# Attention and a token-mixing MLP in one stream: max tiles moved from the projection stretches to the first MLP product

## The chip, the cores and the metric

The kernel runs on one core of a Trainium2 chip. The metric is the device time of one execution in microseconds (us). All engines of the core take part: TensorE (PE; its weight loads are shown as PEld), VectorE (DVE), ScalarE (ACT), GpSimd (POOL) and SyncE (SP), which issues the transfers.

## The reference

The output is a gated sum of two branches over the same x of 2048 tokens by 640 channels, in float32.

```python
g = sigmoid((x * gate_w).sum(-1, keepdims=True))
# branch A: 32 query heads of width 20 on one shared key and value head
q = (x @ wq).reshape(B, S, 32, 20).transpose(0, 2, 1, 3); k = x @ wk; v = x @ wv
p = softmax(einsum("bhqd,bkd->bhqk", q, k) * 20 ** -0.5)
a = einsum("bhqk,bkd->bhqd", p, v).transpose(0, 2, 1, 3).reshape(B, S, 640) @ wo
# branch B: an MLP along the token axis, F = 1728
h = layernorm(x)
u = gelu(einsum("bsd,sf->bdf", h, w1) + b1)
b = (einsum("bdf,fs->bds", u, w2) + b2).transpose(0, 2, 1)
return g * a + (1 - g) * b
```

## The kernel before

The matmuls run on float32 operands split into a high and a low part, so most products are three matmuls (high by high, low by high, high by low), and the contraction is often cut into two halves of 64 rows. PE then works as two row halves side by side; the text calls each a lane. Two matmuls on different lanes run at the same time.

The kernel first projects q, k and v and normalizes x (up to line 438). Then `mix_kernel` writes out by hand one stream of stretches for the rest. A **visit** is one key block of 128 tokens for one unit of four heads and 512 queries; there are 32 units of 16 visits, 512 visits. A visit has four score tiles (`qk`, the matmul of line 700, 512 columns, two per lane), each followed by an exp on ScalarE (line 709) from PSUM to SBUF, and a PV group (`pv_group`, line 735: per visit eight records of 32 output columns). Before a unit's scores come its row maxima: 64 **max tiles** per unit (`ms_next`, the matmul of line 488 with a `tensor_reduce` on VectorE, line 494); they are gathered per unit by `ms_done`, and stored and fetched through DRAM (`store_max`, `fetch_max`). They need no exp and belong to no visit, so they can stand anywhere ahead of their unit.

A **stretch** is what stands between two PV groups: scores and max tiles, and **filler** matmuls of 320 columns from the MLP or the output projection. The filler of a stretch goes on one lane, and most scores and maxes on the other; the next stretch swaps the lanes. The list `ph` holds the filler of every stretch in order:

- the first MLP product, `b1_jobs` (line 986): 84 stretches of 24 filler matmuls, the first of them without visits; each output tile takes four stretches, then `gelu` on ScalarE and GpSimd in steps that `settle` hands out;
- the second product, `b2_jobs` (line 802): 16 row tiles of eight stretches with 20 or 21 fillers;
- the output projection, `a_jobs` (line 931): `NA` blocks of four stretches with 15 fillers;
- the tail: the last `TAIL` visits in `BLOCKS` of two, with no max tiles; here the remaining blocks of the projection are done by `tail_job` (line 886), whole ones first, then those of the last 512 queries for the heads that are ready.

`visits` says how many visits end each stretch (0, 1 or 2). In a stretch the order of score (s) and max (m) tiles on the one lane and around the filler (F) on the other is a letter pattern by visits and filler count (`PATTERN`), shortened or lengthened to a number of max tiles that `shares` hands out. `main` then merges both lanes by planned durations and the planned time at which a PSUM bank comes free. Seven banks rotate among scores, maxes and PV sums (three "ms", three "s", one "o"); an eighth, "g", holds the filler's sum. Outside the tail each PV group's sum is copied from PSUM by ScalarE (line 747) and added by GpSimd (line 748); in the tail it stays in its bank.

The weights w1 and w2 come in chunks of up to four row groups of 128 (`w1_load`, four raw buffers), and `w1_upto` splits each with two GpSimd operations (lines 126 and 127, four split buffers). All transfers named here are issued by SP, in program order. `tail_load` fetches operands of the tail's projection into room that the MLP has left.

Of the kernel before, what the change touches and what calls it, by code (L numbers as in the profile page):

```python
# [27 lines left out]
NU = NQB * NQ  # L28
PRO = 7
LEAD = 46  # L30
TAIL = 24
BLOCKS = (2,) * 12
NA = 10
NP = 12
EPS = 1e-5
GC = math.sqrt(2.0 / math.pi)
# [4 lines left out]
def mix_kernel(ctx: ExitStack, tc: tile.TileContext, A_x, A_wq, A_wk, A_wv, A_wo,  # L41
               B_x, B_w1, B_b1, B_w2, B_b2, gate_w, out):
    nc = tc.nc
    x = A_x[0]
# [39 lines left out]
    HS = NS // 4  # L84
    chunks = [(fc, hf) for d in range(2) for fc in range(FC) for hf in range(4)]
    W2 = len(chunks)
    chunks += [(st, hf) for st in range(NS) for hf in range(4)]
    w1t = {}
    fetched = [0]

# [2 lines left out]
    def w1_load(n):  # L93
        while len(w1raw) < min(n, len(chunks)):
            c = len(w1raw)
            wr = w1r.tile([P, HS, P], F32, name="wr")
            if c < W2:
                fc, hf = chunks[c]
                rows = slice(hf * HS * P, (hf + 1) * HS * P)
                for o in range(0, P, P if fc < FC - 1 else FT):  # L100
                    fw = P if fc < FC - 1 else FT
                    nc.sync.dma_start(out=wr[:, :, o:o + fw],
                                      in_=B_w1[rows, fc * P:fc * P + fw].rearrange("(c p) f -> p c f", p=P))
            else:
                st, hf = chunks[c]
                cols = slice(st * P, (st + 1) * P)
                nf = min(HS, FC - 1 - hf * HS)
                nc.sync.dma_start(out=wr[:, :nf, :],
                                  in_=B_w2[hf * HS * P:(hf * HS + nf) * P, cols].rearrange("(c p) s -> p c s", p=P))
                if nf < HS:  # L110
                    for o in range(0, P, FT):
                        nc.sync.dma_start(out=wr[o:o + FT, nf, :], in_=B_w2[(FC - 1) * P:, cols])
            w1raw[c] = wr

    def w1_upto(n):
        while fetched[0] < min(n, len(chunks)):
            c = fetched[0]
            w1_load(c + 1)
            wr = w1raw[c]
            wh = w1p.tile([P, HS, P], F32R, name="wh")  # L120
            wl = w1p.tile([P, HS, P], F32R, name="wl")
            nv = min(HS, FC - HS * chunks[c][1]) if c >= W2 else HS
            if c < 4 * PRO + 4:
                nc.scalar.activation(wh, wr, AF.Copy)  # L124
            else:
                nc.gpsimd.tensor_copy(wh[:, :nv], wr[:, :nv])
            nc.gpsimd.tensor_sub(wl[:, :nv], wr[:, :nv], f32(wh[:, :nv]))  # L127
            w1t[c] = wh, wl
            fetched[0] += 1
            w1_load(c + 4)  # L130
# [19 lines left out]
    qtiles, qmax = {}, {}  # L150
# [18 lines left out]
    with tc.tile_pool(name="pa", bufs=1) as pa, \  # L169
# [622 lines left out]
    def b2_jobs(st):  # L792
        hold = {}

        def mm(fc, k, d, half):
            if not hold.get("n"):
                hold["p"], hold["n"] = ps_g.tile([P, NB], F32, name="g"), 0
            wh, wl = w1t[W2 + 4 * st + fc // HS]
            w, u = ((wh, u_hi), (wh, u_lo), (wl, u_hi))[k]
            hold["n"] += 1  # L800
            r = slice(64 * half, 64 * half + 64)
            other_tile(half, nc.tensor.matmul(hold["p"][:, :HD2], w[r, fc % HS, :], u[d][r, fc, :],  # L802
                             start=(hold["n"] == 1), stop=(hold["n"] == 6 * FC - 3)))
# [12 lines left out]
        def steps(d):  # L816
            full = [[(fc, k), (fc, k)] for fc in range(FC - 1) for k in range(3)]
            return [[lambda fc=fc, k=k, h=h: mm(fc, k, d, h) for h, (fc, k) in enumerate(f)]
                    for f in full + [[(FC - 1, 0), (FC - 1, 1)], [(FC - 1, 2)]]]

        return (lambda: None), [(steps(d), lambda d=d: done(d)) for d in range(2)]

# [172 lines left out]
    def batches(tiles, counts):  # L995
        out = []
        for n, (load, parts, *_) in enumerate(tiles):
            for d, (steps, done) in enumerate(parts):
                cnt = counts.pop(0)
                rows = [[f[h] for f in steps if len(f) > h] for h in range(2)]  # L1000
                cut = [[len(r) * j // cnt for j in range(cnt + 1)] for r in rows]
                for j in range(cnt):
                    rest = []
                    if d == 0 and j == 0 and n + 1 < len(tiles):
                        rest.append(tiles[n + 1][0])
                    out.append(([r[c[j]:c[j + 1]] for r, c in zip(rows, cut)], rest, [done] if j == cnt - 1 else []))
        return out
# [11 lines left out]
    for st in range(NS):  # L1019
        ph += stretches(batches([b2_jobs(st)], [2] * 2))  # L1020
        if st < NS - 1:
            for k, n in ((-3, 1), (-1, 4)):
                ph[k][1].append(lambda c=W2 + 4 * (st + 1) + n: w1_upto(c))
    ph[-1][1].append(second)
    for c in range(DC):
# [2 lines left out]
    aj = [a_jobs(st) for st in range(NA)]  # L1028
    ph[-8][1].append(aj[0][0])
    ph += stretches(batches(aj, [1] * 2 * NA))  # L1030
    visits = [0] + [2] * (len(ph) - 4 * NA - 1)
    left = len(units) - TAIL - sum(visits)
    visits += [1] * (8 * NA - left) + [2] * (left - 4 * NA)
    assert len(visits) == len(ph)
    early = NS - 4 - NA + 4
    for i in range(early):
        ph[len(ph) - 3 - 2 * (early - 1 - i)][1].append(lambda i=i: tail_load(i))
# [14 lines left out]
    sent, back_in = {0}, {0}  # L1052

    AHEAD, DRAIN, ENTER, FIRST = 4, 0.19, 0.138, 0.1
    PATTERN = {(2, 24): ("smsmsssmsmmsmmms", "F"), (2, 20): ("smsmssmmsmmssm", "mFs"), (2, 15): ("smsmsssmsmmss", "mFmm"),
               (1, 15): ("msmmssms", "F"), (0, 24): ("mmmmmmmssss", "Fs")}

    def pattern(k):
        return PATTERN[visits[k], min((n for n in (15, 20, 24)), key=lambda n: abs(n - len(ph[k][0])))]

    def shares():
        base = [sum(x.count("m") for x in pattern(k)) for k in range(len(ph))]
        total, got, at = 64 * NU - sum(given), [], 0
        for k in range(len(ph)):
            at += base[k]
            got.append(total * at // sum(base))
        return [e - s for s, e in zip([0] + got, got)]

    lanes = [0.0, 0.0]
    fresh = [True, True]  # L1070
# [7 lines left out]
    def main(k, vs, n_max):  # L1078
# [5 lines left out]
        xs, side = pattern(k)  # L1084
        before, after = side.split("F")
        need = end + AHEAD - sc[b]
        n_m = n_max - (before + after).count("m")
        while xs.count("s") < need:
            i = len(xs) * 2 // 3
            xs = xs[:i] + "s" + xs[i:]  # L1090
        while xs.count("s") > need and xs.count("s") > 0 and vs and need >= 0 and (k + 1 < len(ph)):
            i = xs.rindex("s")
            xs = xs[:i] + xs[i + 1:]
            break
        while xs.count("m") < n_m:
            xs += "m"
        while xs.count("m") > max(0, n_m):
            i = xs.rindex("m")
            xs = xs[:i] + xs[i + 1:]
        xs, before, after = list(xs), list(before), list(after)  # L1100
        while sc[1 - b] + (before + after).count("s") < end:
            before.append("s")
        total, count = len(xs) + len(before) + len(after) + len(fs), 0
        while fs or after or before or xs:
            if count == (total + 1) // 2:
# [24 lines left out]
        settle(len(vs) == 2)  # L1130
        if vs:
            n, kb = units[vs[0]][0] + 1, units[vs[0]][1]
            if n in kept and n not in back_in:
                fetch_max(n)
                back_in.add(n)
        for f in rest:
# [14 lines left out]
    pool.append((0.0, ps_o.tile([P, NB], F32, name="o")))  # L1151
    v = 0
    clock.update(now=0.0, act=0.0, dve=0.0, pv=0.0)
    share = shares()
    for k in range(len(ph)):
        n = visits[k]
        main(k, list(range(v, v + n)), share[k])
        v += n
        if k == len(ph) - 4:
            raw = last_wo()  # L1160
        if k == len(ph) - 2:
            w_last = split_last(raw)
# [130 lines left out]
```

## Time and profile before

| what | value |
|---|---|
| median of 3 runs (lowest, highest) | 1635.69 us (1635.39, 1635.93) |
| profiled execution | 1635.82 us |
| its span | 1634.0 us |
| ScalarE, GpSimd: share of the span | 80%, 53% |
| DMA | 135.88 MB, mean 83 GB/s |
| VectorE max tiles (line 494, largest group) | 682 ns each |
| ScalarE exps (line 709, largest group) | 619 ns each |

The span is the time from the first to the last instruction of the profiled execution; the rest of its 1635.82 us lies around it. A mean duration on VectorE or ScalarE runs from start to end of one instruction, and the next one may start before that, so the distance of starts has to be read from the order of time. A matmul's recorded duration also overlaps its neighbours'; a row with "x2" merges two. In the order of time a bracket gives the idle time ahead of an instruction and what ended it.

### The profile page before, as it was taken

How to read it: one execution, taken by the hardware profiler on the slowest of the kernel's cores; microseconds unless marked ns; L12 is line 12 of the kernel's file. 1: busy time of each engine (PE TensorE's matmuls, PEld its weight loads, DVE VectorE, ACT ScalarE, POOL GpSimd, SP SyncE). 2: the span in 40 equal slices, each digit the busy share in tenths (PEclk: the TensorE clock that was granted, in tenths of full speed). 3: DMA queues.
4: the chain of work that ended last, by engine and by line, in shares of the span. 5: the costliest groups of instructions: out<-in, count | busy, mean ns of one | idle time of the engine just before them, and what ended most of it. 6: DMA issues, size and time to landing. Idle time of an engine off the chain costs nothing.

```text
span 1634.0 us, 39357 instructions
## 1 busy us (share of the span) xinstructions
PE 1623.5 (99%) x14877; PEld 1133.6 (69%) x14877; DVE 1395.2 (85%) x2396; ACT 1304.3 (80%) x2579; POOL 873.2 (53%) x986
## 2 busy tenths in 40 slices
PE   9999999999999999999999999999999999999998
PEld 7899667767677676666666666666666666666666
DVE  6689888888888888888898998999888898799943
ACT  4445888888888888888888888888888888888885
POOL 6568677777787777434444444544344443433320
PEclk9999999999999999999999999999999999999999
DMA  7655222222332222122221222112222212334321
GB/s 214 209 164 145 65 79 78 73 66 69 86 82 71 79 74 69 38 65 73 65 72 52 71 64 70 57 45 57 65 65 64 65 54 85 102 97 144 117 79 40
DMA packets 173603, 135.88 MB, mean 83 GB/s; under 512 B 32793, under 2 KB 139446, under 8 KB 173414
## 3 DMA queue, kind: packets, MB, share of 16 engines
q1 hardware_dynamic: 173126, 133.04, 28.7%
q8 instruction: 117, 1.92, 0.5%
q14 instruction: 72, 0.59, 0.1%
q10 hardware_dynamic: 288, 0.33, 0.1%
HBM read 100.27 MB, written 31.65 MB: 81 GB/s over the span
## 4 chain that ended last, share of the span: by engine, by line
PE 94%; ACT 5%; issue 1%; DVE 0%; DVEq 0%; ACTq 0%
PE s L735 14%; PE g L802 11%; PE ms L735 11%; PE ms L700 9%; PE s L700 8%; PE g L986 7%; PE ms L488 6%; PE s L488 6%; PE pp L296 4%; ACT p L709 4%; PE o L735 4%; PE pu L621 3%; PE o L700 3%; PE g L931 3%; PE o L488 2%; PE ml L488 1%
## 5 line engine op out<-in xcount | busy, mean ns | idle before, releaser
L494 DVE TENSOR_REDUCE mp<-ms 128x1 f32<-128x512 f32 x842 | 554.7, 682 | 65.8 <-PE ms L488 51.8
L494 DVE TENSOR_REDUCE mp<-s 128x1 f32<-128x512 f32 x823 | 542.9, 682 | 66.1 <-PE s L488 55.1
L709 ACT ACTIVATE p<-ms 128x512 f32<-128x512 f32 x894 | 522.8, 619 | 35.8 <-PE s L735 14.4
L709 ACT ACTIVATE p<-s 128x512 f32<-128x512 f32 x861 | 504.7, 620 | 36.8 <-PE ms L735 14.1
L748 POOL TENSOR_TENSOR acc<-acc,part 128x512 f32<-128x512 f32 x220 | 284.6, 1294 | 349.0 <-ACT part L747 344.4
L700 PE MATMUL ms<-qst,kst 62*128 62x512 f32 x894 | 352.8, 411 | 0.0
L700 PE MATMUL s<-qst,kst 62*128 62x512 f32 x861 | 340.4, 411 | 0.0
L488 PE MATMUL ms<-kst,qmx 60*128 60x512 f32 x842 | 328.9, 410 | 0.0
L488 PE MATMUL s<-kst,qmx 60*128 60x512 f32 x823 | 320.3, 409 | 0.5 <-DVE yo L544 0.5
L986 PE MATMUL g<-slot,wh 64*128 64x320 f32 x1344 | 307.6, 313 | 1.3 <-ACT p L709 1.0
L986 PEld LDWEIGHTS g<-slot,wh 64*128 64x128 f32 x1344 | 221.1, 184 | 70.5 <-issue 66.2
L735 PE MATMUL s<-p,v_sb 128*32 128x512 f32 x2056 | 248.1, 599 | 1.1
L127 POOL TENSOR_TENSOR wl<-wr,wh 128x512 fp32r<-128x512 f32 (+1 forms) x176 | 218.1, 1239 | 29.4 <-ACT wh L124 9.7
L494 DVE TENSOR_REDUCE mp<-o 128x1 f32<-128x512 f32 x291 | 198.1, 681 | 19.4 <-PE o L488 15.2
L700 PEld LDWEIGHTS ms<-qst,kst 62*128 62x128 f32 x894 | 164.1, 185 | 66.5 <-ACT p L709 55.3
L986 PE MATMUL g<-slot,wl 64*128 64x320 f32 x672 | 205.2, 305 | 0.0
L802 PE MATMUL g<-slot,wh 64*128 64x320 f32 x864 | 199.2, 312 | 0.0
L700 PEld LDWEIGHTS s<-qst,kst 62*128 62x128 f32 x861 | 158.8, 185 | 57.9 <-ACT p L709 46.3
L802 PE MATMUL g<-u,wh 64*128 64x320 f32 x864 | 198.7, 312 | 0.0
L735 PE MATMUL ms<-p,v_sb 128*32 128x512 f32 x1512 | 182.3, 598 | 1.0
L709 ACT ACTIVATE p<-o 128x512 f32<-128x512 f32 x280 | 173.1, 618 | 10.7 <-PE ms L735 4.2
L488 PEld LDWEIGHTS ms<-kst,qmx 60*128 60x128 f32 x842 | 154.2, 185 | 8.0 <-ACT p L709 1.0
(248 smaller groups left out, 3147.6 us busy)
## 6 DMA issues: line engine op xcount, KB each, us to landing
wr<-in_B_w_dram SPq DMA_DIRECT2D x152, 256.0 KB
qmx<-q_scr SPq DMA_DIRECT2D x192, 80.0 KB
qst<-q_scr SPq DMA_DIRECT2D x192, 80.0 KB
slot<-o_scr SPq DMA_DIRECT2D x20, 320.0 KB
y_scr<-yo SPq DMA_DIRECT2D x16, 320.0 KB
o_scr<-ot SPq DMA_DIRECT2D x124, 40.0 KB
o_scr<-acc SPq DMA_DIRECT2D x124, 40.0 KB
q_scr<-qh SPq DMA_DIRECT2D x19, 256.0 KB
```

Source lines behind the costliest of these rows:

```text
L127: nc.gpsimd.tensor_sub(wl[:, :nv], wr[:, :nv], f32(wh[:, :nv]))
L296: nc.tensor.matmul(pp, w, t, start=first and n == 0, stop=not more and n == len(steps) - 1)
L488: nc.tensor.matmul(ms, qmax[n][64 * b:64 * b + 60, pr, qt * P:(qt + 1) * P], kst[64 * b:64 * b + 60, kq * NB:(kq + 1) * NB], start=True, s ...
L494: r = nc.vector.tensor_reduce(mtiles[n][:, c, kq:kq + 1], ms, axis=AX.X, op=ALU.max)
L621: nc.tensor.matmul(pu[r][:, :HD2], w[rows, c, :], h[rows, st, :], start=(st == 0 and k == 0), stop=(st == NS - 1 and k == 2))
L700: nc.tensor.matmul(s, kst[64 * b:64 * b + 62, kb * P:(kb + 1) * P], q[64 * b:64 * b + 62, pr, :], start=True, stop=True)
L709: e = nc.scalar.activation(p, s, AF.Exp, scale=SCALE)
L735: nc.tensor.matmul(o[32 * hh:32 * hh + 32, :], v_sb[:, kb + i, :], ptiles.pop((u, hh)), start=opened and i == 0, stop=(i == len(us) - 1) a ...
L748: nc.gpsimd.tensor_add(sums[0], sums[0], part)
L802: other_tile(half, nc.tensor.matmul(hold["p"][:, :HD2], w[r, fc % HS, :], u[d][r, fc, :], start=(hold["n"] == 1), stop=(hold["n"] == 6 * F ...
L931: other_tile(half, nc.tensor.matmul(hold["p"][:, :HD2], o[r, c, :], w[r, c, d * HD2:(d + 1) * HD2], start=(hold["n"] == 1), stop=(hold["n" ...
L986: other_tile(half, nc.tensor.matmul(hold["p"][:, :HD2], w[r, st % HS, :], h[d][r, st, :], start=(hold["n"] == 1), stop=(hold["n"] == 6 * NS)))
```

## The change

The projection takes 8 blocks in the loop and leaves two more to the tail, which has 26 visits in 13 blocks in place of 24 in 12. All stretches but the first now end with two visits; before, 14 of the 40 projection stretches ended with one. The letter patterns are new, one for each filler count: those of the first product allow nine max tiles (one of them behind the filler on the other lane), those of the projection six; `share` fixes the max tiles of each lane per stretch by these patterns and takes one off in every fourth stretch of the first product where the lanes would have too many. The stretches of 21 fillers get a pattern of their own.

The four chunks of a w2 row tile hold 4, 3, 3 and 4 row groups in the order 0-3, 11-13, 4-6, 7-10 (before: 4, 4, 4, 2 in order), the second product runs through them in that order, and two of the four are split after the sixth of the eight stretches of the row tile before, two after its last (before: one and three). The odd half step of the last row group goes to the other lane in the second half of the channels.

```diff
-TAIL = 24
-BLOCKS = (2,) * 12
-NA = 10
+TAIL = 26
+BLOCKS = (2,) * 13
+NA = 8
...
-    chunks += [(st, hf) for st in range(NS) for hf in range(4)]
+    W2_FC = ((0, 1, 2, 3), (11, 12, 13), (4, 5, 6), (7, 8, 9, 10))
+    place = {fc: (j, i) for j, fcs in enumerate(W2_FC) for i, fc in enumerate(fcs)}
+    chunks += [(st, j) for st in range(NS) for j in range(4)]
...
-            full = [[(fc, k), (fc, k)] for fc in range(FC - 1) for k in range(3)]
-            return [[lambda fc=fc, k=k, h=h: mm(fc, k, d, h) for h, (fc, k) in enumerate(f)]
-                    for f in full + [[(FC - 1, 0), (FC - 1, 1)], [(FC - 1, 2)]]]
+            pairs = []
+            for fc in (fc for fcs in W2_FC for fc in fcs):
+                if fc < FC - 1:
+                    pairs += [[(fc, k), (fc, k)] for k in range(3)]
+                else:
+                    pairs += [[(fc, 0), (fc, 1)], [(fc, 2), None][::1 - 2 * d]]
+            return [[f and (lambda fc=f[0], k=f[1], h=h: mm(fc, k, d, h)) for h, f in enumerate(fs)] for fs in pairs]
...
-            for k, n in ((-3, 1), (-1, 4)):
+            for k, n in ((-3, 2), (-1, 4)):
...
-    visits = [0] + [2] * (len(ph) - 4 * NA - 1)
-    left = len(units) - TAIL - sum(visits)
-    visits += [1] * (8 * NA - left) + [2] * (left - 4 * NA)
-    assert len(visits) == len(ph)
+    visits = [0] + [2] * (len(ph) - 1)
+    assert sum(visits) == len(units) - TAIL
...
-    PATTERN = {(2, 24): ("smsmsssmsmmsmmms", "F"), (2, 20): ("smsmssmmsmmssm", "mFs"), (2, 15): ("smsmsssmsmmss", "mFmm"),
-               (1, 15): ("msmmssms", "F"), (0, 24): ("mmmmmmmssss", "Fs")}
+    PATTERN = {24: ("smssmsmmssmssmmm", "Fm"), 20: ("smsmssmmsmmssm", "mFs"), 21: ("smsmsmmssmmsmsm", "Fs"),
+               15: ("smsssmmmssms", "mFs"), 0: ("mmmmmmmmmmssss", "Fsmm")}
...
-    def shares():
-        base = [sum(x.count("m") for x in pattern(k)) for k in range(len(ph))]
-        total, got, at = 64 * NU - sum(given), [], 0
-        for k in range(len(ph)):
-            at += base[k]
-            got.append(total * at // sum(base))
-        return [e - s for s, e in zip([0] + got, got)]
+    base = [[pattern(k)[int(k % 2 != h)].count("m") for k in range(len(ph))] for h in range(2)]
+
+    def share(k):
+        left = [32 * NU - x for x in given]
+        if k >= m:
+            return [(x * c[k] + sum(c[k:]) // 2) // sum(c[k:]) for x, c in zip(left, base)]
+        over = [sum(c[k:]) - x for x, c in zip(left, base)]
+        h = over.index(max(over))
+        return [c[k] - (i == h and k % 4 == 1 and over[h] > 0) for i, c in enumerate(base)]
```

The rest of the diff makes `w1_load`, `w1_upto` and `b2_jobs` follow the new chunks, makes `main` keep the max tiles of each lane to `share`, and lets it fetch a unit's maxima only once its q tile is there.

More of the change, by code (lines that the diff above doesn't have):

```diff
@@ L104, in w1_load @@
             else:
-                st, hf = chunks[c]
+                st, j = chunks[c]
                 cols = slice(st * P, (st + 1) * P)
-                nf = min(HS, FC - 1 - hf * HS)
+                first, nf = W2_FC[j][0], len(W2_FC[j]) - (FC - 1 in W2_FC[j])
                 nc.sync.dma_start(out=wr[:, :nf, :],
-                                  in_=B_w2[hf * HS * P:(hf * HS + nf) * P, cols].rearrange("(c p) s -> p c s", p=P))
-                if nf < HS:
+                                  in_=B_w2[first * P:(first + nf) * P, cols].rearrange("(c p) s -> p c s", p=P))
+                if nf < len(W2_FC[j]):
                     for o in range(0, P, FT):
@@ L121, in w1_upto @@
             wl = w1p.tile([P, HS, P], F32R, name="wl")
-            nv = min(HS, FC - HS * chunks[c][1]) if c >= W2 else HS
+            nv = len(W2_FC[chunks[c][1]]) if c >= W2 else HS
             if c < 4 * PRO + 4:
@@ L797, in mm @@
                 hold["p"], hold["n"] = ps_g.tile([P, NB], F32, name="g"), 0
-            wh, wl = w1t[W2 + 4 * st + fc // HS]
+            j, i = place[fc]
+            wh, wl = w1t[W2 + 4 * st + j]
             w, u = ((wh, u_hi), (wh, u_lo), (wl, u_hi))[k]
@@ L801, in mm @@
             r = slice(64 * half, 64 * half + 64)
-            other_tile(half, nc.tensor.matmul(hold["p"][:, :HD2], w[r, fc % HS, :], u[d][r, fc, :],
+            other_tile(half, nc.tensor.matmul(hold["p"][:, :HD2], w[r, i, :], u[d][r, fc, :],
                              start=(hold["n"] == 1), stop=(hold["n"] == 6 * FC - 3)))
@@ L999, in batches @@
                 cnt = counts.pop(0)
-                rows = [[f[h] for f in steps if len(f) > h] for h in range(2)]
+                rows = [[f[h] for f in steps if f[h]] for h in range(2)]
                 cut = [[len(r) * j // cnt for j in range(cnt + 1)] for r in rows]
@@ L1054, in mix_kernel @@
     AHEAD, DRAIN, ENTER, FIRST = 4, 0.19, 0.138, 0.1
-    PATTERN = {(2, 24): ("smsmsssmsmmsmmms", "F"), (2, 20): ("smsmssmmsmmssm", "mFs"), (2, 15): ("smsmsssmsmmss", "mFmm"),
-               (1, 15): ("msmmssms", "F"), (0, 24): ("mmmmmmmssss", "Fs")}
+    PATTERN = {24: ("smssmsmmssmssmmm", "Fm"), 20: ("smsmssmmsmmssm", "mFs"), 21: ("smsmsmmssmmsmsm", "Fs"),
+               15: ("smsssmmmssms", "mFs"), 0: ("mmmmmmmmmmssss", "Fsmm")}
     def pattern(k):
-        return PATTERN[visits[k], min((n for n in (15, 20, 24)), key=lambda n: abs(n - len(ph[k][0])))]
-    def shares():
-        base = [sum(x.count("m") for x in pattern(k)) for k in range(len(ph))]
-        total, got, at = 64 * NU - sum(given), [], 0
-        for k in range(len(ph)):
-            at += base[k]
-            got.append(total * at // sum(base))
-        return [e - s for s, e in zip([0] + got, got)]
+        return PATTERN[len(ph[k][0]) if visits[k] else 0]
+    base = [[pattern(k)[int(k % 2 != h)].count("m") for k in range(len(ph))] for h in range(2)]
[6 more added lines that the diff above has]
+        return [c[k] - (i == h and k % 4 == 1 and over[h] > 0) for i, c in enumerate(base)]
     lanes = [0.0, 0.0]
@@ L1086, in main @@
         need = end + AHEAD - sc[b]
-        n_m = n_max - (before + after).count("m")
-        while xs.count("s") < need:
+        if xs.count("s") < need:
             i = len(xs) * 2 // 3
-            xs = xs[:i] + "s" + xs[i:]
-        while xs.count("s") > need and xs.count("s") > 0 and vs and need >= 0 and (k + 1 < len(ph)):
+            xs = xs[:i] + "s" * (need - xs.count("s")) + xs[i:]
+        elif xs.count("s") > need:
             i = xs.rindex("s")
             xs = xs[:i] + xs[i + 1:]
[L1094 to L1097, printed above, removed]
+        if xs.count("m") < n_max[b]:
+            xs += "m" * (n_max[b] - xs.count("m"))
+        while xs.count("m") > n_max[b]:
             i = xs.rindex("m")
             xs = xs[:i] + xs[i + 1:]
+        after += "m" * (n_max[1 - b] - (before + after).count("m"))
+        while (before + after).count("m") > n_max[1 - b]:
+            if "m" in after:
+                after = after.replace("m", "", 1)
+            else:
+                before = before.replace("m", "", 1)
+        before = "s" * (end - sc[1 - b] - (before + after).count("s")) + before
         xs, before, after = list(xs), list(before), list(after)
-        while sc[1 - b] + (before + after).count("s") < end:
-            before.append("s")
         total, count = len(xs) + len(before) + len(after) + len(fs), 0
@@ L1132, in main @@
             n, kb = units[vs[0]][0] + 1, units[vs[0]][1]
-            if n in kept and n not in back_in:
+            if n in kept and n in qtiles and n not in back_in:
                 fetch_max(n)
@@ L1153, in mix_kernel @@
     clock.update(now=0.0, act=0.0, dve=0.0, pv=0.0)
-    share = shares()
     for k in range(len(ph)):
         n = visits[k]
-        main(k, list(range(v, v + n)), share[k])
+        main(k, list(range(v, v + n)), share(k))
         v += n
```

## The prediction

> **What bounds the kernel now.** I read the page's busy shares first, then the table by stage (cut at the starts of PV groups, the matmuls of line 735), then the order of time inside single stretches. The columns of the stage table are PE, PEld, DVE, ACT and POOL busy us, each with its count.
>
> ```profile
> PE 1623.5 (99%) x14877; PEld 1133.6 (69%) x14877; DVE 1395.2 (85%) x2396; ACT 1304.3 (80%) x2579; POOL 873.2 (53%) x986
> ```
>
> ```profile
> 167.89:648.13 480.24, 477.84 (x4593) 335.97 (x4591) 424.40 (x706) 393.96 (x799) 354.03 (x417) 1.00 0.28 74
> 648.13:1366.50 718.37, 718.33 (x6690) 483.09 (x6689) 649.07 (x1105) 612.07 (x1188) 319.09 (x350) 1.00 0.21 61
> 1366.50:1416.03 49.53, 48.73 (x445) 33.19 (x444) 36.09 (x61) 43.24 (x79) 22.86 (x23) 1.00 0.37 117
> 1426.20:1559.98 133.78, 133.78 (x1129) 85.25 (x1128) 122.71 (x210) 112.86 (x228) 53.40 (x60) 1.00 0.40 120
> 1559.98:1620.66 60.68, 60.68 (x598) 39.17 (x597) 17.23 (x32) 48.23 (x97) 5.42 (x8) 1.00 0.14 42
> ```
>
> The rows are: the first product (82 stretches, 5.86 us each), the second (128, 5.61), the projection's 14 one-visit stretches (3.54), its last 24 two-visit stretches (5.57; two more lie between the rows), and the tail (12 blocks, 5.06). The clock column is 1.00 in all. The two projection rows and the gap between them are 1366.50 to 1559.98, 193.48 us. PE is "busy" all the time, so its share decides nothing. I asked what starts each PV group. In a stretch of the first product:
>
> ```profile
> 383.71 0.39 PE L700 MATMUL o<-qst,kst 62*128 62x512 f32 x1
> 383.76 0.45 PE L986 MATMUL g<-slot,wh 64*128 64x320 f32 x2
> 383.94 0.39 PE L488 MATMUL s<-kst,qmx 60*128 60x512 f32 x1
> ...
> 384.49 0.30 PE L986 MATMUL g<-slot,wl 64*128 64x320 f32 x1
> 384.62 0.42 PE L700 MATMUL ms<-qst,kst 62*128 62x512 f32 x1
> 384.98 1.92 PE L735 MATMUL s<-p,v_sb 128*32 128x512 f32 x16
> 386.83 0.41 PE L986 MATMUL g<-slot,wh 64*128 64x320 f32 x1
> ```
>
> Two row halves (lanes) run side by side. A 512-column tile (score or max; X below) follows the last on its lane by 0.234 us (383.71, 383.94); between 383.76 and 384.49 stand five 320-column matmuls (F; the omitted rows hold the other three), 0.147 each. The PV group holds 384.98 to 386.83, 1.85 us. One lane has 16 X = 3.74 us, the other 24 F = 3.53. The longer lane, about 0.1 for its start and 0.1 before PV, plus 1.85, gives 5.80: **the X lane bounds these stretches**, and the F lane has about 0.2 us to spare, just under one X.
>
> A two-visit projection stretch holds less (8 scores, 8 maxes, 15 F; 13 X on one lane, 3 X and 15 F on the other), so lanes end at 3.14 and the stretch should last 5.1. It lasts 5.57. Why:
>
> ```profile
> 1483.80 0.50 PE L700 MATMUL s<-qst,kst 62*128 62x512 f32 x1
> ...
> 1486.36 0.45 PE L488 MATMUL o<-kst,qmx 60*128 60x512 f32 x1
> 1486.59 0.50 PE L700 MATMUL s<-qst,kst 62*128 62x512 f32 x1
> 1486.91 0.49 PE L488 MATMUL s<-kst,qmx 60*128 60x512 f32 x1
> 1487.08 0.49 PE L700 MATMUL ms<-qst,kst 62*128 62x512 f32 x1
> 1487.51 1.92 PE L735 MATMUL s<-p,v_sb 128*32 128x512 f32 x16
> ```
>
> ```profile
> 1484.37 0.69 DVE L494 TENSOR_REDUCE mp<-ms 128x1 f32<-128x512 f32 x1 [0.69 <-PE ms L488]
> ...
> 1486.17 1.28 DVE L494 TENSOR_REDUCE mp<-s 128x1 f32<-128x512 f32 x2
> 1487.37 0.68 DVE L494 TENSOR_REDUCE mp<-ms 128x1 f32<-128x512 f32 x1
> ```
>
> The last X start 0.2 to 0.3 apart on both lanes together, no longer in the lanes' rhythm, and PV writes bank "s" at 1487.51, just after the second of the two maxes from 1486.17 has read an "s" (it starts at 1486.77 and takes 0.68, to 1487.45). Maxes follow each other by 0.60. So **PSUM banks bound the projection stretches**: seven rotate, one must be free for PV, six may be unread; of 16 tiles ten must be read first, and the fifth max is the tenth.
>
> **The change part by part.** In the built order of the changed kernel 64 of the 82 stretches hold 9 maxes and 18 hold 8; all 32 projection stretches hold 6 maxes and 8 scores; there are 13 tail blocks, with 432 F in place of 312. The same X, F and visits are done; only their places change.
>
> (1) *Projection.* 40 stretches become 32, all of two visits. Lanes: 12 X = 2.81 against 15 F and 2 X = 2.67. Banks: 14 tiles, so eight must be read by PV. The fourth max is read at 0.57 (1484.37 less 1483.80) + 3 x 0.60 + 0.68 = 3.05 after the start, and the fourth exp earlier. Lanes and banks agree on PV at 3.05 to 3.1, so a stretch of 4.95; I add 0.08 for DVE's other work and the ScalarE evacuation of the projection's bank: 5.03. 32 x 5.03 = 161, and an allowance of 0.4 for the stage's first stretch: 161.4 against 193.5, **-32**. Ends: 4.93 (lanes alone) gives -35.7; no shrinking, 5.57, gives -15.2. I take the value near the first, because what set 5.57 was the fifth max, and two maxes go.
>
> (2) *Tail.* Two more blocks are projected here. 312 F / 12 = 26.0 a block, 432 / 13 = 33.2. The tail row's 60.68 / 12 = 5.06 is 8 X and 26 F shared by two lanes (2.85), 1.85 and 0.36 around them. Each lane gets 3.6 F more: 3.6 x 0.147 = 0.53, so 5.59 a block, 13 x 5.59 = 72.7: **+12**. If the F filled waits it would be 13 x 5.06, +5; unshared between lanes, 13 x 6.12, +19. ScalarE is busy 48.23 of 60.68 and DVE 17.23, so neither hides or holds it; I take the lanes.
>
> (3) *The ninth max in 64 stretches of the first product.* On PE it goes behind the 24 F: 3.53 + 0.23 = 3.76 against the other lane's 3.74, so nearly free. DVE must have room:
>
> ```profile
> 167.89:648.13 480.24, 407.10 (x656) 1.00 0.28 74
> ```
>
> ```profile
> 381.80 0.69 DVE L494 TENSOR_REDUCE mp<-s 128x1 f32<-128x512 f32 x1 [0.78 <-PE s L488]
> 382.40 2.69 DVE L494 TENSOR_REDUCE mp<-ms 128x1 f32<-128x512 f32 x4
> 385.01 0.68 DVE L494 TENSOR_REDUCE mp<-s 128x1 f32<-128x512 f32 x1
> 385.61 0.68 DVE L494 TENSOR_REDUCE mp<-ms 128x1 f32<-128x512 f32 x1
> ```
>
> 656 maxes are 8 a stretch; DVE is busy 424.40 / 82 = 5.18 of 5.86 and idle 0.68, nearly all ahead of a stretch's first max. One more at the start spacing of 0.60 (385.01, 385.61) leaves 0.08. Banks: of 17 tiles 11 must be read. The stretch that starts at 381.02 (1.85 after the PV at 379.17 of the rows below) has its first max 0.78 later; the fifth is read at 0.78 + 4 x 0.60 + 0.68 = 3.86, and the sixth exp about 3.7 (below), just ahead of the lanes' 3.95. It fits with nothing to spare, and DVE's other work (17.3 us, 0.2 a stretch on average, up to 1 us at once) will push it at times. Ends: 0, and 64 x 0.60 = +38 if DVE's idle time can't be filled. I take 0.07 each, **+4.5**, nearer the first because the idle time ends with the first tile's arrival and the extra max would be read ahead of that.
>
> [...]
>
> (4) *The 18 with 8 maxes* are every fourth, where a GELU tanh stands between the exps:
>
> ```profile
> 373.18:379.17 5.99, 5.87 (x58) 4.10 (x57) 5.16 (x10) 4.70 (x11) 3.81 (x4) 1.00 0.35 97
> 379.17:384.98 5.81, 5.81 (x57) 4.12 (x57) 4.91 (x9) 4.75 (x10) 3.56 (x7) 1.00 0.50 84
> ```
>
> ```profile
> 378.11 0.51 ACT L549 ACTIVATE yo<-yo 128x320 f32<-128x320 f32 x1
> 378.47 1.13 ACT L709 ACTIVATE p<-s 128x512 f32<-128x512 f32 x2
> ```
>
> ```profile
> 381.65 1.08 ACT L709 ACTIVATE p<-ms 128x512 f32<-128x512 f32 x2
> 382.61 0.62 ACT L709 ACTIVATE p<-o 128x512 f32<-128x512 f32 x1
> ```
>
> Exps follow each other by 0.48 (381.65, 382.61 two later), from 0.63 after the start: the sixth is read at 0.63 + 5 x 0.48 + 0.62 = 3.65; the tanh adds 0.36 and costs 0.18. The new order has the same number of tiles: **0** (ends -3 and +3).
>
> (5) *Second product.* Stretches of 21 F used the order for 20: 21 F and 2 X, 3.55, on one lane. Now 1 X and 21 F, 3.32, against 15 X, 3.51: 32 x 0.04 = -1.3, up to -3.5 where F starts late; **-2**. The w2 blocks (4, 3, 3, 4 row groups) move one of three POOL conversions at a tile's end ahead, and only their order on SP and POOL changes: POOL is busy 319 of 718 us here, PE 718.33 of 718.37, so no wait is there to go: 0. If a block came late PE would wait once per tile, 16 times.
>
> (6) *Start of the loop.* The stretch without visits gets 12 maxes for 7, the next one 8 for 7.
>
> ```profile
> 161.97 1.28 DVE L494 TENSOR_REDUCE mp<-s 128x1 f32<-128x512 f32 x2
> 165.07 0.69 DVE L494 TENSOR_REDUCE mp<-ms 128x1 f32<-128x512 f32 x1 [1.82 <-PE ms L488]
> ```
>
> Six maxes are 3.6 us of DVE; it is idle for 1.8 here, so at most +1.8; **+1**. The added early loads for the tail (two, some 1 MB each) go on SP in the projection, whose DMA share is 0.40: 0.
>
> Sum: -32 + 12 + 4.5 + 0 - 2 + 1 = -16.5. The profiled execution took 1635.82 (span 1634.0), 0.13 over the median, so about **1619.3 us**.
>
> **The rivals.** *A, the ninth max is half hidden:* 0.2 to 0.35 a stretch through banks in place of 0.07, as its slack of 0.08 on DVE suggests: +8 to +18, 1627 to 1637. *B, the projection stays at 5.57* because the exps and not the maxes hold the banks: +17, 1636. Against it: the fifth max ends right at PV. *C, slower:* VectorE becomes the bound of the first product. Each ninth max waits with its bank for a DVE that is still idle at the start of a stretch, and costs its whole 0.60, +38 for +4.5: 1635.8 - 21 + 38 = 1653. It decides from 21 / 64 = 0.33 a stretch on. [...] *D, the change doesn't do what it says:* the built order excludes it for the counts; a late w2 block or tail load remains, some us.
>
> **How the numbers follow.** Forecast 0.66 (1611 to 1627), A 0.15, B 0.05, C 0.11, D and others 0.03. The range 1609 to 1637 holds the forecast's, most of A and B, and leaves C out. A measurement here can tell about 0.2%, 3.3 us: faster (below 1632.4) is the forecast, three quarters of A and a little of D, 0.79; same 0.08 (B, the end of A); slower 0.13 (C, D).
>
> **What would show it.** Projection stretches of 4.95 to 5.1; tail blocks of 5.5 to 5.7; first product stretches with 9 maxes at 5.8 to 5.95, DVE idle in them under 0.2 us; the second product's row shorter by 1 to 4 us. I am wrong if DVE's idle time ahead of a stretch's first max stays near 0.7 with nine maxes (C), or if PV in the projection waits for an exp (B).

## The result and the profile after

The changed kernel takes 1632.24 us (median of 12 runs, 1631.90 to 1632.94) against 1635.84 us for the kernel before on the same chip (12 runs): a ratio of 0.9978, 95% interval 0.9969 to 0.9987. That is 3.6 us faster, 0.22%: little, but the whole interval lies below 1. The forecast was 1619.3, 16.5 us faster; 1632 lies in the range and in rival A.

The table by stage of the changed kernel, cut like that of before at the starts of PV groups, here line 737 (columns: the stretch and its length, then PE, PEld, DVE, ACT and POOL busy us with counts, granted clock, DMA share, GB/s):

```profile
0.00:168.85 168.85, 166.41 (x1289) 143.78 (x1289) 132.54 (x260) 83.27 (x171) 111.95 (x126) 1.00 0.62 179
168.85:663.83 494.98, 494.40 (x4658) 343.99 (x4657) 461.59 (x774) 395.05 (x799) 353.89 (x418) 1.00 0.28 73
663.83:1382.53 718.70, 718.35 (x6691) 480.65 (x6690) 653.02 (x1106) 611.83 (x1188) 317.62 (x348) 1.00 0.23 61
1382.53:1544.66 162.13, 162.13 (x1442) 103.14 (x1441) 125.25 (x212) 152.55 (x305) 64.72 (x70) 1.00 0.43 130
1544.66:1616.69 72.03, 72.03 (x740) 48.80 (x739) 20.95 (x39) 52.25 (x105) 7.73 (x10) 1.00 0.16 50
```

Read against the rows of before, the difference lies in one row:

| stage | before | after | difference | forecast |
|---|---|---|---|---|
| up to the first PV group | 167.89 | 168.85 | +1.0 | +1 |
| first product, 82 stretches | 480.24 | 494.98 | **+14.7** | +4.5 |
| second product, 128 | 718.37 | 718.70 | +0.3 | -2 |
| projection, 40 and 32 | 193.48 | 162.13 | -31.4 | -32 |
| tail, 12 and 13 blocks | 60.68 | 72.03 | +11.4 | +12 |

The span fell by 3.9 us. Projection, tail and start came as worked out, and the first product gave most of it back. By my cut of its matmuls, its 64 stretches with nine maxes last 6.05 us on average, where three of four lasted 5.81 with eight; the 18 with eight, those with the tanh, last 5.98 (6.01 before).

What ends such a stretch? One starts at 394.41. First PE at its end, then ScalarE, then VectorE:

```profile
397.89 0.31 PE L993 MATMUL g<-slot,wl 64*128 64x320 f32 x1
398.03 0.39 PE L490 MATMUL s<-kst,qmx 60*128 60x512 f32 x1
398.18 0.49 PE L490 MATMUL o<-kst,qmx 60*128 60x512 f32 x1
398.60 1.92 PE L737 MATMUL ms<-p,v_sb 128*32 128x512 f32 x16
400.46 0.41 PE L993 MATMUL g<-slot,wh 64*128 64x320 f32 x1
```

```profile
395.08 0.59 ACT L711 ACTIVATE p<-s 128x512 f32<-128x512 f32 x1
395.56 0.61 ACT L711 ACTIVATE p<-o 128x512 f32<-128x512 f32 x1
396.04 0.62 ACT L711 ACTIVATE p<-ms 128x512 f32<-128x512 f32 x1
396.51 1.12 ACT L711 ACTIVATE p<-s 128x512 f32<-128x512 f32 x2
397.47 0.66 ACT L711 ACTIVATE p<-o 128x512 f32<-128x512 f32 x1
```

```profile
394.06 0.68 DVE L496 TENSOR_REDUCE mp<-s 128x1 f32<-128x512 f32 x1
395.17 0.69 DVE L496 TENSOR_REDUCE mp<-s 128x1 f32<-128x512 f32 x1 [0.43 <-PE s L490]
395.87 1.29 DVE L496 TENSOR_REDUCE mp<-ms 128x1 f32<-128x512 f32 x2
397.07 0.68 DVE L496 TENSOR_REDUCE mp<-s 128x1 f32<-128x512 f32 x1
397.67 1.28 DVE L496 TENSOR_REDUCE mp<-ms 128x1 f32<-128x512 f32 x2
```

The weight load of the last tile in this stretch, and of the last tile in the stretch of before that the prediction shows (its matmul at 384.62, PV at 384.98):

```profile
398.18 0.18 PEld L490 LDWEIGHTS o<-kst,qmx 60*128 60x128 f32 x1 [0.18 <-ACT p L711]
```

```profile
384.55 0.18 PEld L700 LDWEIGHTS ms<-qst,kst 62*128 62x128 f32 x1
```

The last filler starts at 397.89, so its lane is free at 398.04. The ninth max starts at 398.18 and writes bank "o", which the sixth exp has read from 397.47 to 398.13. Its weight load waits for that exp too and starts with the matmul; before, it started ahead of it. Of the sixteen tiles ahead of it ten have then been read: six exps and four maxes (the fourth, from 397.07, ends at 397.75; the fifth, from 397.67, would end at 398.35). In 62 of the 64 stretches the last tile starts less than 75 ns after an exp's end; before, in none of 82. VectorE is not full: in this stretch it is still idle for 0.43 ahead of its first max.

### The profile page after: what moved, and what is told of

The parts are those of the page before. It is cut to its first block, busy times and chain, and to the rows that moved or that the text cites. A ratio compares the mean times of both kernels' runs of the same rounds, so it can differ in the third digit from the quotient of the medians.

```text
span 1630.2 us, 39380 instructions
## 1 busy us (share of the span) xinstructions
PE 1622.6 (100%) x14877; PEld 1127.8 (69%) x14877; DVE 1400.5 (86%) x2404; ACT 1297.2 (80%) x2567; POOL 858.5 (53%) x974
## 4 chain that ended last, share of the span: by engine, by line
PE 99%; ACT 0%; DVE 0%; issue 0%; DVEq 0%; ACTq 0%
PE ms L737 14%; PE g L805 11%; PE s L737 11%; PE s L702 9%; PE g L993 9%; PE ms L702 8%; PE ms L490 7%; PE s L490 7%; PE o L737 5%; PE pp L298 4%; PE pu L623 3%; PE o L702 3%; PE o L490 2%; PE g L938 2%; PE ml L490 1%; PE s L893 1%
## 5 line engine op out<-in xcount | busy, mean ns | idle before, releaser
L496 DVE TENSOR_REDUCE mp<-ms 128x1 f32<-128x512 f32 x859 | 566.1, 683 | 69.7 <-PE ms L490 61.9
L711 ACT ACTIVATE p<-s 128x512 f32<-128x512 f32 x906 | 534.2, 624 | 37.8 <-PE s L737 13.1
L711 ACT ACTIVATE p<-ms 128x512 f32<-128x512 f32 x847 | 498.3, 621 | 36.7 <-PE s L737 11.4
L750 POOL TENSOR_TENSOR acc<-acc,part 128x512 f32<-128x512 f32 x212 | 274.4, 1294 | 392.9 <-ACT part L749 373.9
L702 PE MATMUL s<-qst,kst 62*128 62x512 f32 x906 | 353.8, 413 | 0.0
L702 PE MATMUL ms<-qst,kst 62*128 62x512 f32 x847 | 335.5, 413 | 0.4 <-ACT p L711 0.4
L737 PE MATMUL ms<-p,v_sb 128*32 128x512 f32 x1904 | 228.9, 598 | 0.0
L702 PEld LDWEIGHTS s<-qst,kst 62*128 62x128 f32 x906 | 166.7, 185 | 55.1 <-ACT p L711 31.7
L702 PEld LDWEIGHTS ms<-qst,kst 62*128 62x128 f32 x847 | 156.2, 185 | 55.3 <-ACT p L711 43.0
L737 PE MATMUL s<-p,v_sb 128*32 128x512 f32 x1536 | 184.7, 598 | 0.0
```

The costliest lines, as they stand in the source:

```text
L496: r = nc.vector.tensor_reduce(mtiles[n][:, c, kq:kq + 1], ms, axis=AX.X, op=ALU.max)
L702: nc.tensor.matmul(s, kst[64 * b:64 * b + 62, kb * P:(kb + 1) * P], q[64 * b:64 * b + 62, pr, :], start=True, stop=True)
L711: e = nc.scalar.activation(p, s, AF.Exp, scale=SCALE)
L737: nc.tensor.matmul(o[32 * hh:32 * hh + 32, :], v_sb[:, kb + i, :], ptiles.pop((u, hh)), start=opened and i == 0, stop=(i == len(us) - 1) a ...
L750: nc.gpsimd.tensor_add(sums[0], sums[0], part)
```

## The experiments

Theory 1: the ninth max waits for a PSUM bank. Seven rotate, so the seventeenth tile needs ten read, and the tenth is the sixth exp, 3.7 us after the stretch's start; the filler lane is free at 3.63. Theory 2 (the prediction's rival C): VectorE's work is the bound. Theory 3: one more tile on a lane costs PE this time whatever the banks do. All kernels are the changed one with one edit unless said otherwise. The expectations call a tile cold whose matmul is recorded with 0.49 us in place of 0.39.

**The ninth max left out** (`e1_last_out`); `ms_next(b, 0)` writes a constant into the max's column and does nothing else.

```diff
+                    cut = nine and c == "m"
-                    issue(1 - b, X_US, (s_next if c == "s" else ms_next)(1 - b) or (lambda: None), tf)
+                    f = ms_next(1 - b, 0) if cut else (s_next if c == "s" else ms_next)(1 - b)
+                    issue(1 - b, 0.0 if cut else X_US, f or (lambda: None), tf)
```

> The changed kernel with the ninth max left out in the 64 stretches of the first product that have one (its matmul and its reduction; a one-column memset on VectorE stands in its place, so those row maxima miss 512 of 2048 columns). All theories put the loss of the change here: a stretch falls from 6.05 to about 5.81 us, 64 times, so about 1617 us (-15). If the stretches stay near 6.05, something else of the change holds them and no theory stands.

1619.98 us, ratio to before 0.9905 (0.9890 to 0.9919). Its first product:

```profile
170.25:652.83 482.58, 481.97 (x4593) 333.13 (x4593) 426.35 (x774) 395.78 (x799) 353.90 (x418) 1.00 0.29 74
```

12.4 us less than with the ninth max, 0.19 for each of the 64. That doesn't yet say why the tile costs so much. That the total meets the forecast of 1619.3 is chance: the forecast had charged the tile 4.5 us and would have been 1614.8 without. What is over lies mainly in the first product, 2.3 us above before (its next stretch starts 1.89 us after PV in place of 1.86), and in the second, 718.91 where 716.4 was forecast.

**The first max left out in its place** (`e2_first_out`): the same edit on the first "m" of the other lane.

> The changed kernel with the first max of the same 64 stretches left out and the ninth kept behind the filler (matmul and reduction of the first are left out, so row maxima miss columns). Theory 1, the ninth max waits for a PSUM bank that the sixth exp frees: with 16 tiles its bank is free, it starts when the filler ends (3.63 us after the stretch's start), PV about 3.97, a stretch of 5.82, about 1617 us (-15). Theory 2, VectorE is the bound: eight reductions again, also 1617. Theory 3, a 512-column tile behind 24 fillers costs PE this time whatever else: the lane is as long as before, 6.05, about 1632 us (0).

1643.09 us, 1.0045 (1.0030 to 1.0060). None of the three theories had said slower. The first product takes 506.0 us, a stretch 6.17, with one max fewer. One handover between two stretches, all engines:

```profile
428.83 0.68 DVE L498 TENSOR_REDUCE mp<-ms 128x1 f32<-128x512 f32 x1
...
429.65 0.38 PE L995 MATMUL g<-slot,wh 64*128 64x320 f32 x1 [0.28 <-DVE mp L498]
429.66 0.49 PE L704 MATMUL ms<-qst,kst 62*128 62x512 f32 x1
```

With the first max gone VectorE gets its first work late (1.24 us into the stretch that starts here, where the changed kernel has 0.77), so its last reduction of a stretch ends late too, here at 429.51. The next stretch's first filler changes lanes in the filler's bank, and by the kernel's own ordering (`other_tile`) it waits for the reduction that follows the last filler: PE was idle 0.28, and 11.2 us in the stage (busy 494.84 of 506.01). From PV to the next stretch's first tile it is now 2.0 to 2.2 us in three of four stretches, where the changed kernel has 1.85. So here it isn't the count of maxes that sets the time but when VectorE gets its tiles.

Inside the 64 stretches, though, PV comes earlier: 4.07 us after the first tile (median), in the changed kernel 4.20. The last tile of the stretch shown, weight load and matmul, and its PV:

```profile
433.29 0.18 PEld L491 LDWEIGHTS s<-kst,qmx 60*128 60x128 f32 x1
433.38 0.40 PE L491 MATMUL s<-kst,qmx 60*128 60x512 f32 x1
433.72 1.92 PE L739 MATMUL o<-p,v_sb 128*32 128x512 f32 x16
```

The max behind the filler starts when the filler ends, here 0.1 later than in the changed kernel, and its weight load 0.09 ahead of it. In the 37 of the 64 stretches with the load 0.06 or more ahead, the matmul is recorded with 0.40 and PV starts 0.33 after it; in the 14 where both start together, 0.49 and 0.42. Theory 3 falls with that: by these numbers a max behind 24 fillers, with its bank free in time, would put PV at 3.63 + 0.34 = 3.97, which is what theory 1 expected, and before the change PV stood at 3.95.

**The matmul without its reduction** (`e3_no_reduce`).

```diff
-            r = nc.vector.tensor_reduce(to, ms, axis=AX.X, op=ALU.max)
+            r = nc.vector.memset(to, -1e30)
```

> The changed kernel with the ninth max's matmul kept at its place and its reduction left out (a one-column memset stands for it, so row maxima miss columns). Theory 1, it waits for a bank that an exp frees: the wait is the same, stretches of 6.0 to 6.05, 1629 to 1632 us (-3 to 0). Theory 2, VectorE is the bound: 0.6 us less of it, stretches of 5.81 to 5.85, about 1617 to 1620 us (-12 to -15). Theory 3, lane time on PE: 1632 us (0).

1630.66 us, 0.9969 (0.9957 to 0.9981).

```profile
169.29:663.03 493.74, 493.74 (x4657) 343.92 (x4656) 426.57 (x774) 394.82 (x799) 354.13 (x418) 1.00 0.28 73
```

VectorE's busy time in the first product falls from 461.59 to 426.57 us, and the nine-max stretches stay at 6.05: the last tile follows an exp's end in 62 of 64. Theory 2, and rival C with it, falls: 35 us of VectorE work were worth 1.2 us, nearly all of it in the 18 stretches with eight maxes (5.92 for 5.98).

**The ninth max ahead of the filler** (`e4_front`).

```diff
-    PATTERN = {24: ("smssmsmmssmssmmm", "Fm"),
+    PATTERN = {24: ("smssmsmmssmssmmm", "mF"),
```

> The changed kernel with the ninth max ahead of the filler on its lane in place of behind it; nothing left out. Theory 1, banks: VectorE starts 0.2 us earlier (a max at the stretch's start), so the tenth tile is read at about 3.65 us in place of 3.72, and no cold tile stands behind the filler: 0.05 to 0.12 us less a stretch, 1624 to 1629 us (-3 to -8). Theory 2, VectorE: its work is the same and starts earlier, 0 to -0.2 a stretch, 1620 to 1632 us. Theory 3, lane time: the lanes hold the same, 1632 us (0).

1628.73 us (1628.25 to 1629.07), 0.9956 (0.9940 to 0.9973): faster than both kernels, 7.0 us under that of before by the medians and 3.5 under the changed one, whose runs don't overlap its runs. The first product takes 492.02 us, a nine-max stretch 6.00. The last tile starts at 3.71 in place of 3.77; its weight load starts just after an exp's end in 30 stretches and just after a max's in 32. So both readers are now about equally late, as theory 1 has it. The tile is still recorded with 0.49.

**ScalarE's copy of the PV sum left out ahead of the nine-max stretches** (`e7_no_copy`).

```diff
-            else:
+            elif copy:  # False where the next stretch has nine maxes
                 part = ev.tile([P, NB], F32, name="part", bufs=2)
```

> The changed kernel without ScalarE's copy of the PV sum (and GpSimd's add) at the start of the stretches with nine maxes, so those visits are missing from the sums; all matmuls, exps and reductions stay. Theory 1, banks: the bank of the PV sum is free at once and the exps start up to 0.2 us earlier, the last tile no longer waits (3.63 in place of 3.77) and doesn't start cold: 5.82 to 5.95 a stretch, 1618 to 1626 us (-6 to -14). Theory 2 (VectorE) and theory 3 (lane time on PE): no change, 6.05 a stretch, 1632 us.

1626.48 us, 0.9944 (0.9930 to 0.9958); first product 489.50 us; nine-max stretches 5.96, just above what theory 1 expected. The sixth exp is read 0.13 earlier, the last tile starts at 3.64, when the filler ends, and PV comes 0.13 earlier. Neither VectorE's work nor the lanes were touched, so theories 2 and 3 don't explain it. The last tile still follows an exp's end in 62 of 64, its weight load starts with it, and it is recorded with 0.50; so PV still follows it by 0.43, where 0.33 is usual with eight maxes (0.32 with the ninth left out).

So what waits for the bank is the tile's weight load. Side by side, for the same 64 stretches, in us after the first tile (medians; by my own cut of the traces):

| kernel | a reader of a bank ends | weight load of the last tile | its matmul | PV |
|---|---|---|---|---|
| before | 3.47 (max) | 3.52 | 3.63 | 3.95 |
| changed | 3.72 (exp) | 3.77 | 3.77 | 4.20 |
| `e2_first_out` | 3.59 (mostly exp) | 3.64 | 3.73 | 4.07 |
| `e4_front` | 3.67 (both) | 3.71 | 3.71 | 4.13 |
| `e7_no_copy` | 3.59 (exp) | 3.64 | 3.64 | 4.07 |

In each the load starts 0.05 after the end of a read, and PV 0.43 after the load. The 0.24 a stretch is thus the load's delay, 3.52 to 3.77: 0.13 or 0.14 of it the matmul waits as well, and the other 0.1 it starts without a load ahead of it.

**The maxes back in the projection** (`e5_maxes_back`): the patterns of before in the changed kernel.

> The changed kernel with the letter patterns of the kernel before, so eight maxes in every stretch of the first product and eight or nine in those of the projection; eight projected blocks, 26 last visits and the w2 groups stay. Nothing is left out. Theory 1, banks: the first product falls back to about 481 us, the projection rises from 162 to 32 x 5.57 = 178 to 181 us, the tail stays at 72: 1632 to 1636 us, so moving the maxes by itself brought 0 to 3 us. Theory 2 or 3 would give the first product the same 481 and say nothing else of the projection; if the projection stayed near 162, the maxes never held it and the whole loss in the first product would be for nothing: about 1619 us.

1634.56 us, 0.9994 (0.9985 to 1.0003). First product, projection and tail:

```profile
168.76:649.56 480.80, 478.35 (x4594) 336.40 (x4592) 424.98 (x707) 394.07 (x799) 353.51 (x417) 1.00 0.29 74
...
1367.94:1548.72 180.78, 180.78 (x1509) 114.69 (x1508) 164.89 (x281) 151.52 (x306) 65.52 (x73) 1.00 0.40 120
1548.72:1621.06 72.34, 72.34 (x742) 49.11 (x741) 21.98 (x41) 51.78 (x103) 6.79 (x10) 1.00 0.16 49
```

So the rest of the change, eight blocks in the loop and 26 last visits above all, brings nothing that can be measured (193.5 to 180.8 in the projection, 60.7 to 72.3 in the tail). Moving the maxes takes 18.7 us off the projection and puts 14.2 on the first product: 4.5 us of the 18.7 are left. It also shows that the maxes did hold the projection: the 26 stretches with eight, 8 scores and 15 fillers last 5.59 us again (5.58 before), those with six 5.07.

**The order for 21 fillers undone** (`e6_order21`).

```diff
-               21: ("smsmsmmssmmsmsm", "Fs"),
+               21: ("smsmssmmsmmssm", "mFs"),
```

> The changed kernel with the order of the 20-filler stretches used for the 21-filler ones, as before the change; w2 groups and the rest stay. If the new order of these 32 stretches works as forecast (-2) and the w2 regrouping costs as much, the second product takes 1 to 3.5 us longer, 720 to 722 us, and the whole 1633 to 1636 us. If the gain of the 21 is given back in the stretch behind (5.69 us there in place of 5.58), the second product stays at 718 to 719 us and the whole at 1632 us.

1633.51 us, 0.9987 (0.9978 to 0.9996); the second product 720.48. The new order is worth 1.8 us, as forecast, and something else costs 2.1. Stretch by stretch it is the fifth of the eight of a row tile, 5.68 for 5.57 before, 16 times.

**The lane change of the odd half step undone as well** (`e10_noswap`, with the ninth max in front and the order for 20).

```diff
-                    pairs += [[(fc, 0), (fc, 1)], [(fc, 2), None][::1 - 2 * d]]
+                    pairs += [[(fc, 0), (fc, 1)], [(fc, 2), None]]
```

> The kernel with the ninth max ahead of the filler, the 20-filler order for the 21-filler stretches, and the odd half step on the same lane for both halves of the channels; w2's new chunks stay. Nothing is left out. Against the run with the 20-filler order and the lane change (720.5 us in the second product): 718.4, as before the change, if the lane change costs the 2 us; 720.5 if the regrouped chunks do. In all 1628.5 to 1631 us.

1630.25 us, 0.9964 (0.9950 to 0.9978); second product 720.23, the fifth stretch still 5.68. The lane change isn't the cause.

**The w2 chunks of before** (`e9_front_groups`, with the ninth max in front).

```diff
-    W2_FC = ((0, 1, 2, 3), (11, 12, 13), (4, 5, 6), (7, 8, 9, 10))
+    W2_FC = ((0, 1, 2, 3), (4, 5, 6, 7), (8, 9, 10, 11), (12, 13))
-            for k, n in ((-3, 2), (-1, 4)):
+            for k, n in ((-3, 1), (-1, 4)):
```

> The kernel with the ninth max ahead of the filler (1628.7 us, second product 718.5), with w2's chunks, the order of the row groups and the split of one and three conversions as before the change; the odd half step still changes lanes and the 21-filler order is the new one. Nothing is left out. If the regrouped chunks cost the 2 us that the second product lacks against the forecast: 716 to 717 us there, 1626 to 1627 in all. If the lane change of the odd half step does: 718.5 and 1628.7, as without this edit. If the old split makes PE wait for a chunk at each row tile: 720 us or more.

1657.49 us, 1.0134 (1.0119 to 1.0149). The second product takes 746 us, 27.4 more than with the new chunks, all of it in the first stretch of 15 of the 16 row tiles (7.42 for 5.57). GpSimd there, and then PE:

```profile
895.79 0.25 POOL L513 TENSOR_SCALAR mm<-mm 128x16 f32<-128x16 f32 x1 [3.06 <-DVE mm L511]
896.11 0.20 POOL L514 CAST mn<-mm 128x16 fp32r<-128x16 f32 x1
896.39 0.23 POOL L515 TENSOR_TENSOR mn<-mm,mn 128x16 fp32r<-128x16 f32 x1
896.58 1.30 POOL L783 TENSOR_TENSOR acc<-acc,ot 128x512 fp32r<-128x512 f32 x1
897.82 0.61 POOL L128 CAST wh<-wr 128x512 fp32r<-128x512 f32 x1
898.51 1.27 POOL L129 TENSOR_TENSOR wl<-wr,wh 128x512 fp32r<-128x512 f32 x1
```

```profile
898.48 0.42 PE L805 MATMUL g<-u,wh 64*128 64x320 f32 x1 [0.36 <-POOL wh L128]
...
899.84 0.41 PE L805 MATMUL g<-u,wl 64*128 64x320 f32 x1 [0.80 <-POOL wl L129]
```

GpSimd waits 3.06 us for a unit's gathered maxima, and the conversion of the tile's second chunk stands behind that in its queue. The conversions begin 4.1 us after the PV group's start. In the kernel before it is 0.2 us, because there the gather falls into the third stretch of a row tile; a row tile is eight stretches of eight maxes, one unit's 64, so the gather keeps its place in all 16 tiles. The moved maxes shift it to the first stretch. The new chunks, with a second one split earlier, hide that.

The lost 2 us of the second product go with the same shift: in `e5_maxes_back`, with the new chunks and the gather back in the third stretch, the fifth stretch is at 5.57 and the stage at 718.38. What in the shift lengthens the fifth stretch was not followed further.

**More max tiles ahead of the loop** (`e8_lead78`).

```diff
-LEAD = 46
+LEAD = 78
```

(with the order of before for 24 fillers, and two q transfers a step, whatever the row).

> The changed kernel with 78 pairs of max tiles in the stage ahead of the loop in place of 46, which takes the ninth max out of all stretches of the first product (eight, in the order of the kernel before). Nothing is left out. All theories: the first product at 480 to 483 us (-12 to -15). The stage ahead of the loop has 38 us of idle VectorE (129 of 168 busy) and 64 more maxes need 38, and 32 pairs need 32 x 0.23 = 7.5 us of both lanes: it gets 8 to 15 us longer. Total 1625 to 1635 us.

1656.51 us, 1.0129 (1.0114 to 1.0145). The first product is at 481.2 as expected; the stage ahead takes 206.8 us, 38 more and not 8 to 15. Its max tiles, in this kernel:

```profile
L496 DVE TENSOR_REDUCE mp<-ml x156: 642/676/691, 99.1 to 194.7; 128x1 f32<-128x512 f32 x156
who waited for it (us, times):
  PEld ml L490: 24.1, 60
```

and the part of the kernel before in which they stand:

```profile
110.00:158.00 48.00, 47.99 (x594) 46.31 (x594) 47.82 (x84) 26.82 (x55) 41.96 (x41) 1.00 0.53 145
```

In `e8_lead78` PE's weight loads waited 24.1 us in all for these reductions. In the kernel before VectorE was busy 47.82 of 48 us in that part; most of its 38 idle us lie ahead of 99, in the projection of q and k, where no max tile is due. I had read a mean over a stage with two limits. Here VectorE is the bound, and 64 maxes cost 64 x 0.6.

## Why the prediction was wrong

- *(1) Projection*, -32: right in size, -31.4, 5.07 a stretch (5.03 forecast). `e5_maxes_back` shows the maxes as what held it, so rival B falls. The working is right in part: PV was put at 3.05 to 3.1, on the fourth max, and comes at 3.22, 0.43 after a last tile that waits for the fourth exp (read at 2.74), in all 32 stretches. The 0.08 added for other work happened to cover most of that.
- *(2) Tail*, +12: right, +11.4 (5.54 a block for 5.59).
- *(3) The ninth max*, 0.07 a stretch and +4.5 in all: **this step failed**; it measured 0.24 against the stretches of before, and 12.4 us came back by leaving the tile out. The step let the tile go "behind the 24 F" by the lanes alone and asked the banks only for PV: "of 17 tiles 11 must be read" by 3.95. It left out that the ninth max itself needs a bank, and so ten tiles read, when its lane is free at 3.63. The numbers were in the step: the sixth exp at about 3.7, the fifth max at 3.86. Put to the tile, they make it 0.1 late. The rest is that its weight load waits as well, which no row of before had shown at that place, though the projection's last tiles, recorded with 0.49 and 0.50, stood in the quoted rows. The 0.07 was meant for VectorE's other work; without the ninth reduction the stretch stays at 6.05. In the kernel before, the last tile's weight load already followed a max's end (3.47, load 3.52), so those stretches stood at their banks and at the X lane at once, where the prediction saw the lane alone. Rival A had the banks and the size, though it argued from VectorE's slack: with the ninth reduction gone, 13.5 of the 14.7 us stay (`e3_no_reduce`). On VectorE the starts stayed 0.60 apart (395.87, and 397.07 two later), as the prediction took them.
- *(3), DVE*: right in one thing: idle time ahead of the first max is filled when a max is left over; it fell to 0.43 in the stretch shown and not to 0.08, because the stretch grew. Rival C is refuted by `e3_no_reduce`.
- *(4) The 18 with eight maxes*: 0 forecast, 5.98 for 6.01 before, right.
- *(5) Second product*: the order was worth its 1.8 us. "Only their order on SP and POOL changes" was wrong as an argument: the moved maxes shift the gather in GpSimd's queue. With that shift go the 2 us that are lost here, by a way not followed, and with the old chunks it would have cost 27 more. So +0.3 was measured for a forecast of -2. The term's 0 for the chunks holds, if at all, only because they cover a wait that another part of the change makes.
- *(6) Start*, +1: right, +1.0.

## What to carry to other kernels

Where PSUM banks rotate, ask of every moved tile at what moment it needs a bank and how many earlier tiles must have been read by then, not only of the step that ends the stretch. Look for room at both readers, not just on the lane: here the ninth max had its lane free at 3.63 us and its bank read at 3.72. Its place in the order mattered too: at the front of the lane it cost less (6.00 us against 6.05 a stretch). Ask also when the tile's weight load gets that bank: here PV started 0.43 us after the load in each kernel of the side-by-side table, and 0.32 to 0.43 after the matmul. A periodic order has a phase: here 72 max tiles left the projection (264 to 192 by the matmuls in the traces), which is not a whole number of units of 64, and a small gather came to stand in front of a conversion in another engine's queue, 16 times over (with the old chunks, 27.4 us).

## What the runs showed of the hardware

In the first product, taking away 35 us of VectorE reductions, where it was 93% busy, moved the stage by 1.2 us (`e3_no_reduce`), and taking one early reduction a stretch away, by which VectorE got its first tile 1.24 us into the stretch shown and not at 0.77, made the stage 11 us slower (`e2_first_out`): how busy VectorE is says little here, and when it gets its first tile of a stretch says much. The weight load of a stretch's last tile waited for that tile's PSUM bank: it started 0.05 us after the end of a read, in the changed kernel in all 64 nine-max stretches (62 times an exp's). A last tile that started together with its weight load was recorded with 0.49 us, and the PV group behind it started 0.42 after it; with the load 0.06 us or more ahead it was 0.40 and 0.33 (`e2_first_out`, 14 and 37 stretches). PV started 0.43 us after the last tile's weight load in before, the changed kernel, `e2_first_out`, `e3_no_reduce`, `e4_front` and `e7_no_copy` alike (medians 0.425 to 0.429), whichever engine had freed the bank; in `e1_last_out`, where the load was 0.2 ahead, 0.53.
